# The relu sums of two batches on GpSimd instead of VectorE, in a fused attention and mixer kernel

## The chip, the cores and the metric

The kernel runs on one core of one Trainium2 chip. The metric is the device time of one execution in microseconds; the profile is of one execution.

## The reference

Attention with a window and a few global keys, then a mixer. q, k and v are 4 batches x 8 heads x 768 positions x 64 values in float32. What is computed, cut to its core:

```
scores = q @ k^T / sqrt(64) + bias(head, distance)   # kept: keys 0..7, and 0 <= row - key < 96
a      = softmax(scores);   x = (a @ v) with heads side by side   # 4 x 768 x 512
h      = x^T @ U @ V;       u = x + h^T                           # U 768x32, V 32x768
out    = u + relu(u @ w_ch1) @ w_ch2                              # 512 -> 2048 -> 512
```

## The kernel before

**Attention** goes by pairs of heads: 16 pairs, i = 4 b + pair. For a pair, `st_S` makes scores in PSUM (columns in three parts c = 0, 1, 2; VectorE adds the bias at L403), `st_E` the exponentials on ScalarE, `st_V(i, hi)` the product with the values. VectorE then scales that product into x_sb (L451) and GpSimd casts it to x16 in 16 bits (L452). `st_M1` multiplies x16 by U on TensorE (L461), `st_MT` turns the product (L478) and VectorE casts it (L479), `st_M3` multiplies by V (L515); VectorE adds that to x (L520), which is u, GpSimd casts it (L523), and a transposing DMA on the SP queue (`st_X`, L504) puts it into uT. GpSimd also casts each pair's v (`cast_v`, L142). VectorE copies a few columns into kA at L340.

**The mixer** goes by groups (b, g): three groups of 256 rows per batch. For batches 1 to 3 the second product is done with 7 products of quarters instead of 8. `mk_up` makes relu values: 8 units a group, each 8 matmuls (L629) and one relu on ScalarE into htr (L634). When half of a group's units are made, `queue_sums(k)` queues four sums of quarters of htr, 128x512 in 16 bits each, in the order s1, s2, s4, s3; s2 is made from s1, s4 from s2. k is 0 or 1, for the first and the second half. `mk_product` makes a product of 8 matmuls (L682) and adds it to x_sb (L687). The products come in the order x1, y1, x2, y2, x3, y3, x4; x2 uses s2, y2 s1, x3 s3, y3 s4, and the first four matmuls of a product use half 0 of a sum, the others half 1. Similar sums of quarters of w_ch2, named t1 to t4, are made once, early. Batch 0's mixer uses plain products (L664).

**The order** of all instructions on each engine is written out by hand. The main loop (from L800) goes over pairs, at a rate of one pair's attention for some nine units of the mixer; `fill(n)` issues n units (one `mk_up`, product or part of a plain product each). After each unit it raises `count` and takes one queued sum if that has become due (two, where more than four wait): a sum queued in a unit is due two units later. `need`, called by a product ahead of its matmuls, takes sums out of the queue until its own are issued. In the pair's step the fourth and fifth calls of `fill` stand behind `st_V(i - 1, 1)`, `cast_v(i)` and `st_S(i, 2)`, and ahead of `st_M1(i - 1)`. All engines work through their own instructions in that order.

Of the kernel before, what the change touches and what calls it, by code (L numbers as in the profile page):

```python
# [20 lines left out]
def kernel(  # L21
# [13 lines left out]
    nc = tc.nc  # L35
    B, H, S, D = q.shape
# [60 lines left out]
    def load_qk(i, behind=None):  # L97

        b, h0 = i // NP, 2 * (i % NP)
        got = []  # L100
        for src, nm in ((q, "qst"), (k, "kst")):
            st = stp.tile([P, 2, NSB, D], FP32, name=nm, tag=nm, bufs=2)
            if behind is not None:
                behind.memset(st[0:1, 0, 0, 0:1], 0.0)
            if i < NPE:
                nc.sync.dma_start(
                    st.rearrange("p h n d -> p h (n d)"),
                    src[b, h0:h0 + 2].rearrange("h (p n) d -> p h (n d)", n=NSB),
                )
            else:  # L110
                nc.sync.dma_start(
                    st.rearrange("p h n d -> p (h n) d"),
                    src[b, h0:h0 + 2].rearrange("h (n p) d -> p (h n) d", p=P),
                )
            got.append(st)
        staged[i] = got
# [10 lines left out]
    def cast_one(i, w, eng):  # L127
        st16 = stp.tile([P, NSB, 2, D], FP16, name=("q16", "k16")[w], tag=("q16", "k16")[w], bufs=2)
        eng.copy(st16.rearrange("p n h d -> p h n d"), staged[i][w])
        cast.setdefault(i, [None, None])[w] = st16  # L130

    def load_v(i):
        b, h0 = i // NP, 2 * (i % NP)
        st = stp.tile([P, 2 * NSB, D], FP32, name="vst", tag="vst", bufs=2)
        nc.sync.dma_start(
            st, v[b, h0:h0 + 2].rearrange("h (n p) d -> p (h n) d", p=P)
        )
        vsts[i] = st

    def cast_v(i):  # L140
        vt = vbuf[i % NVB]
        nc.gpsimd.tensor_copy(  # L142
            vt.rearrange("p n h d -> p h n d")[:, :, :, 0:D],
            vsts.pop(i).rearrange("p (h n) d -> p h n d", h=2),
        )
        vts[i] = vt
# [78 lines left out]
    def load_w1(c):  # L225
        js = slice(c * (DFF // 4), (c + 1) * (DFF // 4))
        nc.gpsimd.dma_start(w1_16[:, :, js], w1v[:, :, js])

    def load_w2(c):
        nc.gpsimd.dma_start(w2_16[:, 4 * c:4 * c + 4], w2v[:, 4 * c:4 * c + 4])  # L230
# [4 lines left out]
    def new_batch(b):  # L235
        xs[b] = xp.tile([P, NSB, DM], FP32, name="x_sb", tag="x_sb", bufs=3)
        tmps[b] = xp.tile([P, DM], FP16, name="tmp16", tag="tmp16", bufs=3)
        uTs[b] = xp.tile([P, NDC, S], FP16, name="uT", tag="uT")
# [60 lines left out]
    def st_A(i):  # L299
        vt = vts[i]  # L300
        vA = vap.tile([P, NSB - 1, 2, D + 1], FP16, name="vA", tag="vA")
        if i < NPE:
            nc.gpsimd.tensor_copy(vA, vt[:, 0:NSB - 1])
            vas[i] = vA
            return
        nc.sync.dma_start(vA[NG:P], vt[NG:P, 0:NSB - 1])
        nc.sync.dma_start(
            vA[0:NG].rearrange("p n h d -> p n (h d)"),
            vt[0:NG, 0:1].rearrange("p n h d -> p n (h d)").broadcast_to(
                (NG, NSB - 1, 2 * (D + 1))  # L310
            ),
        )
        vas[i] = vA
# [9 lines left out]
    def turn(i):  # L323
        stq, stk = cast.pop(i)
        qT = kp.tile([P, S], FP16, name="qT", tag="qT")
        kT = kp.tile([P, S], FP16, name="kT", tag="kT")
        nc.sync.dma_start_transpose(
            kT.rearrange("d (n p) -> d n p", n=NSB), stk.rearrange("p n h d -> p (n h d)")
        )
        nc.sync.dma_start_transpose(  # L330
            qT.rearrange("d (n p) -> d n p", n=NSB), stq.rearrange("p n h d -> p (n h d)")
        )
        qts[i] = qT
        kts[i] = kT
# [74 lines left out]
    def st_S(i, c):  # L409
        s_dve(i, scores(i, c, False))  # L410
# [138 lines left out]

    def queue_sum(name, part, out_, a, b_, op, wait=0):  # L550

        def go():
            nc.vector.tensor_tensor(out_, a, b_, op)  # L553
            have.add((name, part))
        (slow if name[0] == "t" else jobs).append((count[0] + wait, go))

# [29 lines left out]
    def queue_ff(b):  # L586
        for g in range(NFG):
            queue_group(b, g)
        if b == 0:
            for c in range(4):  # L590
                for made in first_ups:
                    ups_q.extend(made[2 * c:2 * c + 2])
# [118 lines left out]

    ahead, held, kept = [0], [True], deque()

    def fill(n):
        for _ in range(n):
            unit()
            count[0] += 1
            for _ in range(2 if len(jobs) > 4 else 1):
                for queue in (jobs, slow):
                    if queue and queue[0][0] < count[0]:  # L720
                        queue.popleft()[1]()
                        break

    def unit():
        down = downs_q and not held[0] and not any(place(w) <= place(downs_q[0][1]) for _, w in ups_q)
        room = ups_q and (not downs_q or place(ups_q[0][1]) - place(downs_q[0][1])
                          < (3 if held[0] else 2))
        if down and (ahead[0] > 0 or not room):
            ahead[0] = 0
            downs_q.popleft()[0]()  # L730
        elif room:
            ahead[0] = 1
            ups_q.popleft()[0]()
# [66 lines left out]
    for i in range(NP, NPAIR + 2):  # L800
        b, hp = divmod(i, NP)
        live = i < NPAIR
        units = iter(
            (0, 1, 1, 2, 1, 1, 1, 1, 1) if i == NP
            else (0, 1, 1, 1, 1, 1, 1, 1, 1) if i + 1 < NPE
            else (1, 1, 1, 2, 1, 1, 1, 1, 1)
        )
        held[0] = i < NP + 3
        if hp == 0 and live and b + 1 < B:
            new_batch(b + 1)  # L810
        if live and i > NP:
            st_S(i, 0)
        if NPE <= i + 1 < NPAIR:
            turn(i + 1)
        if i + 1 < NPAIR and i != NP + 2:
            load_v(i + 1)
        if i + 2 < NPE:
            load_qk(i + 2)
        fill(next(units))
        if NPE + 2 <= i + 2 < NPAIR:  # L820
            cast_one(i + 2, 1, nc.scalar)
        if NP < i <= NPAIR:
            st_V(i - 1, 0)
        if i == NP:
            load_w1(2)
        if i + 1 < NPE:
            st_T(i + 1)
        if i == NP:
            load_w1(3)
        fill(next(units))  # L830
        if live:
            st_S(i, 1)
        fill(next(units))
        if NP < i <= NPAIR:
            st_V(i - 1, 1)
        if live:
            cast_v(i)
            st_A(i)
        if NPE + 2 <= i + 2 < NPAIR:
            cast_one(i + 2, 0, nc.scalar)  # L840
        if NPE <= i + 3 < NPAIR and i != NP + 2:
            load_qk(i + 3)
        if i > NP + 1 and (i - 2) % NP == NP - 1:
            queue_ff((i - 2) // NP)
            ahead[0] = 1
        if i == NPAIR + 1:
            break
        fill(next(units))
        if live:
            st_S(i, 2)  # L850
        fill(next(units))
        if i > NP:
            st_M1(i - 1)
        else:
            for xo, o, rb in later:
                nc.vector.tensor_tensor(xo, o, rb, ALU.mult)
        if i == NP + 1:
            load_w2(0)
            load_w2(1)
        if i + 2 < NPE:  # L860
            cast_qk(i + 2, nc.gpsimd)
        if live:
            st_E(i, 0)
            if i < NPE:
                st_P(i)
        fill(next(units))
        if i >= NPE:
            for _ in range(min(2, len(kept))):
                kept.popleft()()
        if i > NP:  # L870
            st_MT(i - 1)
        if NPE <= i + 1 < NPAIR:
            st_K(i + 1)
        fill(next(units))
        if i > NP:
            st_M3(i - 1)
        if live:
            st_E(i, 1)
        fill(next(units))
        if i == NP + 1:  # L880
            load_v(i + 2)
            load_qk(i + 4)
        if i > NP:
            st_X(i - 1)
        if i == NP + 1:
            load_w2(2)
            load_w2(3)
        if NPE <= i + 2 < NPE + 2:
            cast_qk(i + 2, nc.gpsimd)
        fill(next(units))  # L890
# [38 lines left out]
```

## Time and profile before

| what | value |
| --- | --- |
| time, median of the runs (least, most) | 232.01 us (231.02, 558.6), 3 runs |
| profiled execution: time, span | 231.95 us, 230.2 us |
| TensorE busy | 220.5 us, 96% |
| VectorE busy | 159.8 us, 69% |
| ScalarE busy | 124.8 us, 54% |
| GpSimd busy | 73.9 us, 32% |
| mean granted TensorE clock | 1.00 |
| sums of relu values (L553, 72 on VectorE), the fastest | 0.41 us each |

The span runs from the first to the last instruction; the execution's own time lies 1.75 us above it. In the text PE is TensorE, PEld its loads of weights, DVE VectorE, ACT ScalarE, POOL GpSimd; L553 is line 553 of the kernel. A timeline row has its start in us from the span's start, its length in us, the engine, the line, the operation with output and inputs, and in brackets the idle time of that engine before it and what ended it. A group's row has the number of instructions, then busy us and mean ns, then the idle time before them. Idle time of an engine costs nothing in itself; time counts where TensorE waits.

### The profile page before, as it was taken

To read this page: it belongs to the slowest core of one execution; us is meant where nothing else is said; L and a number is where in the kernel's file an instruction comes from. 1 tells how busy PE (TensorE), PEld (TensorE's weight loads), DVE (VectorE), ACT (ScalarE), POOL (GpSimd) and SP (SyncE) were. 2 spreads that over 40 slices of the span, in tenths; PEclk is the share of its full clock that TensorE was granted. 3 is DMA by queue.
4 is the path that set the end of the run, shared out by engine and by line. 5 is a ranking of instruction groups with operands and counts; after the bars stand their busy time and mean duration, and the time that the engine had idled before them with its cause. 6 is when DMAs were issued, how large, how long until landed. Compare 5 with 4: busy or idle time off the path is not lost.

```text
span 230.2 us, 5875 instructions
## 1 busy us (share of the span) xinstructions
PE 220.5 (96%) x2418; PEld 171.1 (74%) x2420; DVE 159.8 (69%) x337; ACT 124.8 (54%) x193; POOL 73.9 (32%) x118
## 2 busy tenths in 40 slices
PE   7889999999999999999999999999999999999993
PEld 2445678788744445887888878888988888888882
DVE  3687866658577979597989897989764344444452
ACT  6676757776805253868485857292733434333320
POOL 6399928287553322123313131313111000000000
PEclk9999999999999999999999999999999999999999
DMA  6999999969998979897989993961221202010022
GB/s 188 288 290 245 260 278 188 313 135 163 195 194 181 207 174 251 192 245 175 257 221 196 245 202 99 119 184 28 86 71 36 94 0 94 0 65 28 9 85 93
DMA packets 86563, 36.68 MB, mean 159 GB/s; under 512 B 74152, under 2 KB 83592, under 8 KB 86536
## 3 DMA queue, kind: packets, MB, share of 16 engines
q1 hardware_dynamic: 81480, 32.01, 57.4%
q0 software_dynamic: 5056, 4.29, 12.7%
q8 instruction: 19, 0.31, 0.6%
q14 instruction: 8, 0.07, 0.1%
HBM read 27.46 MB, written 6.29 MB: 147 GB/s over the span
## 4 chain that ended last, share of the span: by engine, by line
PE 66%; DMA 11%; DVE 10%; POOL 4%; ACT 4%; issue 2%; SPq 1%; ACTq 0%; POOLq 0%
PE hps L629 25%; PE cx L682 13%; PE cy L682 10%; PE cps L664 8%; DMA w<-in_moe_w_ch_dram 6%; DMA vst<-in_v_dram 4%; DVE sp L403 3%; PE sc L365 3%; DMA qst<-in_q_dram 2%; ACT ep L415 2%; DVE x_sb L451 2%; PE ob L432 2%; PE sc L515 1%; DVE s L553 1%; PE ob L428 1%
## 5 line engine op out<-in xcount | busy, mean ns | idle before, releaser
L629 PE MATMUL hps<-uT,w 128*128 128x256 f16 x756 | 96.0, 273 | 0.0
L634 ACT ACTIVATE htr<-hps 128x512 f16<-128x512 f32 x96 | 56.4, 598 | 58.4 <-PE hps L629 58.1
L629 PEld LDWEIGHTS <-w 128*128 128x128 f16 x756 | 70.6, 98 | 9.9 <-issue 0.2
L403 DVE SCALAR_TENSOR_TENSOR sp<-sc,relcat 128x1024 f32<-128x1024 f32 (+1 forms) x36 | 40.7, 1131 | 9.1 <-ACT ep L415 4.8
L415 ACT ACTIVATE ep<-sp 128x1408 f16<-128x1408 f32 x24 | 33.1, 1380 | 0.7 <-DVE sp L403 0.6
L452 POOL CAST x<-x_sb 128x384 f16<-128x384 f32 x30 | 16.1, 538 | 48.5 <-DVE x_sb L451 44.3
L682 PEld LDWEIGHTS <-htr 128*128 128x128 f16 x288 | 27.6, 98 | 3.6
L687 DVE TENSOR_TENSOR x_sb<-cx,x_sb 128x256 f32<-128x256 f32 x36 | 15.2, 422 | 18.3 <-PE cx L682 17.7
L664 PE MATMUL cps<-w,htr 128*128 128x512 f16 x96 | 24.0, 379 | 0.4 <-DMA w<-in_moe_w_ch_dram 0.4
L523 POOL CAST x<-x_sb 128x768 f16<-128x768 f32 x12 | 11.0, 915 | 40.8 <-DVE x_sb L520 37.2
L682 PEld LDWEIGHTS <-s 128*128 128x128 f16 x216 | 20.2, 98 | 2.9 <-DVE s L553 0.6
L687 DVE TENSOR_TENSOR x_sb<-cy,x_sb 128x256 f32<-128x256 f32 x27 | 11.4, 422 | 12.5 <-PE cy L682 12.3
L365 PEld LDWEIGHTS <-kT 64*128 64x128 f16 x192 | 8.3, 93 | 13.7 <-issue 12.4
L451 DVE TENSOR_TENSOR x_sb<-ob,rcp 128x384 f32<-128x384 f32 x30 | 16.7, 557 | 1.0
L365 PE MATMUL sc<-qT,kT 64*128 64x128 f16 x192 | 16.8, 221 | 0.3 <-DVE x_sb L520 0.2
L432 PE MATMUL ob<-v,ep 128*128 128x65 f16 x192 | 16.5, 193 | 0.0
L432 PEld LDWEIGHTS <-ep 128*128 128x128 f16 x192 | 13.9, 98 | 2.3 <-issue 0.4
L142 POOL CAST v<-vst 128x768 f16<-128x768 f32 x16 | 14.0, 877 | 3.9 <-DMA vst<-in_v_dram 3.9
L428 PE MATMUL ob<-vA,ep 128*128 128x65 f16 x160 | 14.4, 194 | 0.4 <-DVE vA L316 0.2
L664 PEld LDWEIGHTS <-htr 128*128 128x128 f16 x96 | 8.4, 97 | 8.5 <-issue 0.5
L520 DVE TENSOR_TENSOR x_sb<-sc,x_sb 128x768 f32<-128x768 f32 x12 | 11.5, 955 | 4.6 <-PE sc L515 4.6
L372 PE MATMUL sc<-qT,kA 64*128 64x128 f16 x160 | 14.2, 217 | 0.3
(108 smaller groups left out, 311.1 us busy)
## 6 DMA issues: line engine op xcount, KB each, us to landing
qst<-in_q_dram SPq DMA_DIRECT2D x16, 384.0 KB, 4.6
kst<-in_k_dram SPq DMA_DIRECT2D x16, 384.0 KB, 6.3
vst<-in_v_dram SPq DMA_DIRECT2D x16, 384.0 KB, 4.5
out_dram<-x_sb SPq DMA_DIRECT2D x23, 256.0 KB, 3.1
w<-in_moe_w_ch_dram POOLq DMA_DIRECT2D x8, 512.0 KB, 9.0
vA<-v SPq DMA_DIRECT2D x8, 152.3 KB, 3.6
out_dram<-x_sb SPq DMA_DIRECT2D x2, 128.0 KB
uT<-x SPq DMA_TRANSPOSE x12, 3.1
```

Of the source, the lines that this page charges most:

```text
L365: nc.tensor.matmul(scs[hi][:, o:o + P], kT[r, kb * P:(kb + 1) * P], qT[r, kb * P:(kb + 1) * P], start=(o == 0 and not on_pe), stop=(o + P ...
L403: nc.vector.scalar_tensor_tensor(out=sps[i][:, :, c0:c0 + tot], in0=both[:, :, 0:tot], scalar=qk_scale / slope[2 * (i % NP)], in1=relfs[c0 ...
L415: nc.scalar.activation(eps[i][:, hi], sps[i][:, hi], AF.Exp, scale=slope[2 * (i % NP)])
L428: nc.tensor.matmul(ob[:, qi], ep[:, OF[qi - 1]:OF[qi - 1] + P], vA[:, qi - 1, hi], start=True, stop=False,)
L432: nc.tensor.matmul(ob[:, qi], ep[:, DG[qi]:DG[qi] + P], vt[:, qi, hi], start=(qi == 0), stop=True,)
L451: nc.vector.tensor_tensor(xo, ob[:, :, 0:D], rb, ALU.mult)
L452: nc.gpsimd.tensor_copy(x16, xo)
L629: nc.tensor.matmul(hps[:, k * FT:(k + 1) * FT], w1_16[:, dc, jt * P:(jt + 1) * P], uT[:, dc, ts], start=(dc == 0 and k == 0), stop=(dc == ...
L634: nc.scalar.activation(cell["htr"][:, 2 * jp:2 * jp + 2].rearrange("p j t -> p (j t)"), hps, AF.Relu)
L664: nc.tensor.matmul(cps, htr[:, jc, t * P:(t + 1) * P], w2_16[:, jc], start=(b > 0 and jc == 0), stop=(jc == NJC - 1),)
L682: nc.tensor.matmul(ps, cell[a][:, j], weight(w, j), start=(first and j == 0), stop=(done is not None and j == HJ - 1), skip_group_check=True,)
L687: nc.vector.tensor_tensor(x_sb[:, n, cs], ps, x_sb[:, n, cs], ALU.add)
```

## The change

The sums of relu values of batches 1 and 2 (`name[1] < B - 1`, B is 4) are issued on GpSimd; those of batch 3 and the sums of weights stay on VectorE. `fill` gets a second argument; two calls of the main loop pass False, and then no queued sum is taken after the unit.

```diff
     def queue_sum(name, part, out_, a, b_, op, wait=0):
 
+        eng = nc.gpsimd if name[0] != "t" and name[1] < B - 1 else nc.vector
+
         def go():
-            nc.vector.tensor_tensor(out_, a, b_, op)
+            eng.tensor_tensor(out_, a, b_, op)
             have.add((name, part))
...
-    def fill(n):
+    def fill(n, sums=True):
         for _ in range(n):
             unit()
             count[0] += 1
+            if not sums:
+                continue
             for _ in range(2 if len(jobs) > 4 else 1):
...
-        fill(next(units))
+        fill(next(units), False)
         if live:
             st_S(i, 2)
-        fill(next(units))
+        fill(next(units), False)
         if i > NP:
             st_M1(i - 1)
```

## The prediction

> **What bounds the kernel now.** I read the page first: busy times, then the groups by line, then the table of stretches, the waits from 88 us on, and the timeline around the sums.
>
> ```profile
> PE 220.5 (96%) x2418; PEld 171.1 (74%) x2420; DVE 159.8 (69%) x337; ACT 124.8 (54%) x193; POOL 73.9 (32%) x118
> ```
>
> TensorE is busy for 220.5 of 230.2 us. The sums that move exist from 96 us on, so what counts is how much TensorE waits there. The table of stretches has, after the stretch and its length, the busy time of PE, PEld, DVE, ACT and POOL:
>
> ```profile
> 111.00:122.00 11.00, 11.00 (x139) 9.26 (x135) 9.78 (x21) 8.03 (x12) 3.01 (x4) 1.00 0.95 230
> 122.00:133.00 11.00, 11.00 (x137) 9.33 (x137) 9.77 (x21) 7.54 (x11) 2.76 (x4) 1.00 1.07 223
> 133.00:145.00 12.00, 11.72 (x147) 9.55 (x145) 10.39 (x21) 7.54 (x11) 2.97 (x5) 1.00 0.68 141
> ```
>
> VectorE is busy for 9.8 of 11 us here and GpSimd for 3, which makes the move look cheap. But TensorE has no gap: from 89 to 220 us it idles 0.6 us in all. The waits (us in all, times, the longest) say which part of that VectorE's load causes:
>
> ```profile
> PEld L682 <- DVE s L553: 0.6, 1, 0.6
> PE cx L682 <- DVE s L553: 0.3, 1, 0.3
> PE sc L515 <- DVE tmp L479: 0.2, 1, 0.2
> ```
>
> One wait of TensorE for a sum (0.28 us; its weights came 0.56 us late) and one of 0.21 us for the cast at L479. Freeing VectorE can return about half a microsecond; any new wait of TensorE is paid in full.
>
> **What changes, part by part.**
>
> (1) 48 of the 72 sums (six groups of eight) move to GpSimd, those of batch 3 stay.
>
> ```profile
> L553 DVE TENSOR_TENSOR s<-htr 128x512 f16<-128x512 f16 x18 | 8.1, 453 | 3.3 <-ACT htr L634 3.3
> ...
> L294 POOL COPY kA<-kT 128x640 f16<-128x640 f16 x3 | 2.2, 722 | 5.0 <-DVE kT L277 5.0
> ...
> L195 POOL TENSOR_SCALAR rel<-relB 8x128 bf16<-8x128 f32 x1 | 0.5, 537 | 1.0 <-ACT rel L198 1.0
> ```
>
> VectorE sheds 48 x 0.46 = 22 us. No row has a two-operand operation on GpSimd, so its price **d** is bounded. Below: the undisturbed casts took 0.51 us for 384 elements and 0.83 us for 768, that is 0.19 us fixed and 0.83 ns an element (the copy of 640: 0.19 + 0.53 = 0.72, as measured). One operand of 512 would be 0.62 us. Above: the only arithmetic on GpSimd, L195, took 0.537 us for 128 elements; all of what exceeds 0.19 us taken per element (2.7 ns) gives 1.58 us. Between them, reading both operands one after the other at the copy's rate gives 0.19 + 2 x 0.43 = 1.04 us, and two whole passes 1.24 us. I take 1.15, between these two, since a sum is nearest to two copies. The Trainium skill (GPSIMD Engine Reference, Performance versus the Vector engine) speaks against the move: its two inputs share one read port, and 2048 elements take 4497 ns, so by an estimate from that 1.12 us here, which would lower the sum below by 0.4 us; no run so far shows it.
>
> (2) GpSimd works in order, and its casts stand in the same queue: two of 0.51 us a pair at L452 (their x16 feeds st_M1's U product), one of 0.84 at L142, one of 0.83 at L523. What counts is when the second operand half of product x2 is ready. Its eight matmuls use half 0 of s2, then half 1: the fifth starts 0.44 us after the first. Half 1 needs s1 and s2, one after the other: 2d.
>
> (3) The two fills that take no sums (between st_V hi = 1 and st_M1) shift the emission. I followed the counts: a unit raises `count`, a sum becomes due two units after its relu, one is taken a unit (two with over four waiting). In groups (1,0), (1,2) and (2,1) the s1 and s2 of half 1 fall due just in those two fills. They are skipped, and `need` then issues both directly ahead of x2. In GpSimd's queue they stand behind the second x16 cast and, in batch 1's two groups, behind cast_v. In (1,1) and (2,0) they come behind the L523 cast. Only (2,2), beside which no attention is left, has time: relu at 181.6, two sums to 183.9, x2's fifth matmul 184.8.
>
> ```profile
> 102.98 0.64 POOL L452 CAST x<-x_sb 128x384 f16<-128x384 f32 x1 [2.50 <-DVE x_sb L451]
> ...
> 103.86 1.03 PE L682 MATMUL cx<-t,s 128*128 128x256 f16 x8
> ...
> 118.85 0.95 POOL L523 CAST x<-x_sb 128x768 f16<-128x768 f32 x1 [3.59 <-DMA vA<-v]
> ...
> 120.95 1.03 PE L682 MATMUL cx<-t,s 128*128 128x256 f16 x8
> ...
> 135.87 0.51 POOL L452 CAST x<-x_sb 128x384 f16<-128x384 f32 x1 [1.93 <-DVE x_sb L451]
> 136.08 0.57 DVE L553 TENSOR_TENSOR s<-htr 128x512 f16<-128x512 f16 x1
> 136.32 1.03 POOL L142 CAST v<-vst 128x768 f16<-128x768 f32 x1
> ...
> 137.68 0.61 PE L682 MATMUL cx<-t,s 128*128 128x256 f16 x4 [0.28 <-DVE s L553]
> ```
>
> In the clock of before, with 2d = 2.30 and 0.04 us from an end to TensorE (s ended 137.63, the weights began 137.67):
>
> - (1,0): the x16 cast was ready 102.98 behind sums on VectorE; without them (1.0 us of them ahead of it) GpSimd is the limit: L523 to 96.92, s1 and s2 to 99.2, a cast from 99.6, s4 and s3 to 102.4. Cast to 102.9, cast_v to 103.75, sums to 106.05. x2's fifth matmul is due 104.30: **1.8 late**.
> - (1,1): L523 to 119.68, sums to 121.98, due 121.39: **0.6**.
> - (1,2): cast to 136.38, cast_v to 137.22, sums to 139.52, due 137.22: 2.3, less the 0.46 already lost there: **1.9**.
> - (2,0): L523 (start 152.90) to 153.73, sums to 156.03, due 155.44: **0.6**.
> - (2,1): cast (168.90) to 169.41, sums to 171.71, due 171.06: **0.7**.
>
> Each wait moves what follows by as much, so they add: 5.6, and 5 x 0.04 = 0.2, less the 0.21 us of L479's wait: **+5.6 us**. With d the sum moves as 12d - 8.2 from d = 0.95 up (two sums in four of the chains, four in that of (1,0)).
>
> (4) At no cost: s3 and s4 of half 1 run after x2's pair; x3 comes 3.5 us or more after x2, y3 5 us or more, against 2d = 2.3 for both and a cast. Of the casts ahead of M1, pair 9's starts when s3 ends at 102.4 and is done 0.8 us before M1 at 103.71; the other six meet no sum, since none is issued between them and M1 and the earlier ones are through. The casts of hi = 0 can be up to d late behind a sum, but M1 follows 3.6 us or more after their start. The transposes of st_X follow L523 on SP: pair 11's left SP 131.34 and group (2,0) first read uT at 135.54; s2 ahead of that cast ends before it is due, both move together, and the loads and stores behind it on SP move with TensorE. GpSimd issues no DMA after 54 us. t1 and t3 move by a unit or so on VectorE, long ahead of their use from 104 us on.
>
> The profiled execution took 231.95 us for a span of 230.2, and the median is 232.01. 232.0 + 5.6 = **237.6 us**. A measurement of this kernel can tell about 2%, 4.6 us, from no change; the sum is over that by 1.0 us.
>
> **The rivals.**
>
> (A) Not slower by 2%: GpSimd takes both operands at about the one-operand rate. It decides from d = 1.07 down (12 x 1.07 - 8.2 = 4.6). At d = 0.62 the waits of (1,1), (2,0), (2,1) are gone, (1,0) has 0.3 (the x16 cast is then bound by VectorE, 102.0) and (1,2) 0.8: +0.9, 232.9. For it: f16 and f32 copies cost the same per element, so bytes are not the limit. Against: L195 is dearer than a copy, and two operands are two reads.
>
> (B) GpSimd too slow for its queue: at d = 1.58 the x16 cast of pair 9 ends at 104.3, 0.6 late for M1 at 103.71, which takes its part of x2's wait; the formula gives 10.8, and further casts behind sums up to 1 us more: about 243. For it only L195, a shape on 8 partitions.
>
> (C) A new wait on VectorE: the kA copy at L340 (0.165 us, never beside a sum of GpSimd in this trace) is held by one. What shows such contention: sums of 0.41 us that overlapped a cast took 0.93 to 0.97, and casts went 0.51 to 0.64; L403 from PSUM beside a cast kept 1.23. L340 stands ahead of L520, which frees the sc bank for the next S; the bank is free 0.6 us early. One sum (at most 1.15, of which 0.8 is slack before M3 ends) costs nothing; two in a row cost 0.9 in five pairs: +4.5, 242. The Trainium skill (SBUF — State Buffer, Who interferes with whom) has such copies and GpSimd block each other for a whole instruction; the contended sums above agree with its case of two SBUF operands.
>
> (D) The relief of VectorE is all that shows: TensorE's waits of 0.46 and 0.21 go, 231.3. Against: the emission ahead of x2 is fixed by the counts.
>
> **From these the numbers.** The forecast 0.62 (d from 1.07 to 1.35: 236.6 to 240.0), A 0.19, B 0.10, C 0.07, D 0.02. Range: down into A to d = 0.9 (0.85 + 0.1 + 1.3 + 0.1 + 0.2 = +2.5), up to C's 242: 234.5 to 242. Slower by over 2%: forecast, B and C, 0.79; within 2%: A and most of D, 0.20; faster by over 2%: 0.01, as TensorE's waits from 96 us to the end hold too little for 4.6 us.
>
> **What would show it.** L553 on POOL with 48 instructions and a mean near 1.15 us; waits of PEld and PE at L682 (cx, weights t, operand s) for POOL s, five of them, two near 1.8 and three near 0.65 us; none at L461; DVE near 138 us; TensorE's busy time about the same in a longer span; from batch 3 on the same pace. I am wrong if L682's waits are absent or at other products, if a sum takes under 1 us, or if M1 (L461) or S (L365) waits.

## The result and the profile after

The changed kernel took 237.55 us (median of 4 runs, 236.87 to 238.82) against 232.6 (4 runs): a ratio of 1.0265, 95% interval 1.0222 to 1.0307. Every ratio here compares fast executions alone (the 558.6 us of before, 239.7 us of e5 and 238.11 us of e6 are not among them), so it is not the quotient of the two medians. The profiled execution took 238.82 us with a span of 237.0, 6.8 us over the span before. The lines below have numbers two higher from L553 on and four or more higher from L716 on; L682 is now L684, L687 L689.

Page, busy times, and groups of the sums on GpSimd and of the kA copy (the last row is the copy's group before the change):

```profile
PE 222.3 (94%) x2418; PEld 171.7 (72%) x2420; DVE 143.5 (61%) x289; ACT 124.9 (53%) x193; POOL 126.3 (53%) x166
...
L555 POOL TENSOR_TENSOR s<-htr 128x512 f16<-128x512 f16 x12 | 13.9, 1156 | 2.5 <-ACT htr L636 2.5
...
L340 DVE COPY kA<-kT 128x40 f16<-128x40 f16 x8 | 3.2, 400 | 0.0
```

```profile
L340 DVE COPY kA<-kT 128x40 f16<-128x40 f16 x8 | 1.3, 166 | 0.4 <-DMA kT<-k 0.4
```

The work has moved: GpSimd's busy time rises by 52 us, VectorE's falls by 16. A sum costs GpSimd 1.156 us, its four groups agree within 1 ns. The waits from 88 us on that TensorE and its weight loads have for GpSimd (there were none before):

```profile
PEld L684 <- POOL s L555: 6.6, 5, 2.4
...
PE cx L684 <- POOL s L555: 5.3, 5, 2.2
```

Five waits, all at cx with the operand s: x2. In three of the stretches TensorE idles 1.43, 0.53 and 2.16 us, where before it idled 0.21, 0 and 0.28 (the first row is the one of before that the prediction does not show):

```profile
100.00:111.00 11.00, 10.79 (x134) 8.88 (x132) 9.57 (x22) 7.21 (x11) 2.94 (x4) 1.00 0.87 199
```

```profile
100.00:111.00 11.00, 9.57 (x114) 7.94 (x112) 7.03 (x12) 7.79 (x12) 9.08 (x10) 1.00 0.97 232
...
122.00:133.00 11.00, 10.47 (x132) 8.61 (x129) 8.00 (x15) 7.30 (x11) 8.51 (x10) 1.00 0.91 197
133.00:145.00 12.00, 9.84 (x110) 7.51 (x104) 6.50 (x13) 5.33 (x9) 8.61 (x10) 0.87 0.77 164
```

The timeline around x2 of (1,0) and of (1,2), with the rows of GpSimd and of TensorE's product x2 alone:

```profile
102.44 0.50 POOL L452 CAST x<-x_sb 128x384 f16<-128x384 f32 x1
102.89 0.84 POOL L142 CAST v<-vst 128x768 f16<-128x768 f32 x1
103.68 1.15 POOL L555 TENSOR_TENSOR s<-htr 128x512 f16<-128x512 f16 x1
104.11 0.60 PE L684 MATMUL cx<-t,s 128*128 128x256 f16 x4
104.92 1.16 POOL L555 TENSOR_TENSOR s<-s,htr 128x512 f16<-128x512 f16 x1
106.13 0.61 PE L684 MATMUL cx<-t,s 128*128 128x256 f16 x4 [1.43 <-POOL s L555]
...
138.97 0.61 PE L684 MATMUL cx<-t,s 128*128 128x256 f16 x4
141.74 0.96 PE L684 MATMUL cx<-t,s 128*128 128x256 f16 x4 [2.16 <-POOL s L555]
```

The five pairs s1 and s2 stand in GpSimd's timeline where the prediction has them: behind the x16 cast and cast_v in (1,0) and (1,2), behind the cast of L523 in (1,1) and (2,0), behind the x16 cast in (2,1). Four matmuls of x2 run on half 0, the fifth stands until s2 of half 1 is made. What is lost is the time between the first and the fifth, less the 0.44 us of four matmuls: 106.13 - 104.11 - 0.44 = 1.58 us in (1,0), and by the same rows 0.69 in (1,1), 2.33 in (1,2), 0.70 in (2,0), 0.75 in (2,1); 6.05 in all. (The 5.3 us of the wait table leave out the end of the matmul ahead of it.)

The rest of the difference is the granted clock, which is 0.87 from 133 to 145 us. In smaller stretches of the same trace:

```profile
140.00:142.00 2.00, 0.26 (x2) 0.25 (x3) 0.03 (x1) 0.00 (x0) 1.84 (x3) 0.96 0.91 217
142.00:144.00 2.00, 2.00 (x17) 1.40 (x16) 0.42 (x1) 1.05 (x2) 2.00 (x2) 0.50 0.20 63
144.00:146.00 2.00, 2.00 (x17) 1.58 (x16) 0.44 (x3) 1.81 (x4) 0.03 (x1) 0.68 0.00 0
```

After the longest wait the clock is 0.50 and then 0.68: some 1.6 us lost (half of 2 us and a third of 2). What TensorE no longer loses to VectorE is 0.46 us at x2 of (1,2) and, at the two L515 whose operand L479 cast late, 0.37 and 0.29 us: before, L515 began 1.24 and 1.16 us after the start of the L629 unit ahead of it (106.03 - 104.79, 172.70 - 171.54), where it is 0.87 without a wait and in the trace after. Together: 6.05 of new waits, less 1.12, plus 1.6, and 0.25 from a later start of the whole stage (x2 of (1,0) begins at 104.11 instead of 103.86), 6.8 us, which is the difference of the spans.

Because the first 90 us vary from run to run, with the arrival of w_ch2 among other things (the wait for it is 0.4 us in the trace before, 1.4 after, 1.9 in e4), the profiles are compared below by their **stage**: from the start of the third product of (1,0) to the span's end. Before 230.2 - 103.86 = 126.3 us, after 237.0 - 104.11 = 132.9.

### The profile page after: what moved, and what is told of

Read it like the earlier page. It is cut to its first block, busy times and chain, and to the rows that moved or that the text cites. A ratio compares the mean times of both kernels' runs of the same rounds, so it can differ in the third digit from the quotient of the medians.

```text
span 237.0 us, 5884 instructions
## 1 busy us (share of the span) xinstructions
PE 222.3 (94%) x2418; PEld 171.7 (72%) x2420; DVE 143.5 (61%) x289; ACT 124.9 (53%) x193; POOL 126.3 (53%) x166
## 4 chain that ended last, share of the span: by engine, by line
PE 60%; POOL 16%; DMA 9%; DVE 7%; ACT 3%; issue 2%; SPq 1%; POOLq 0%; ACTq 0%
PE hps L631 23%; PE cx L684 12%; PE cy L684 8%; PE cps L666 8%; DMA w<-in_moe_w_ch_dram 6%; POOL s L555 5%; DMA vst<-in_v_dram 3%; DVE sp L403 2%; ACT ep L415 2%; PE sc L365 2%; POOL v L142 2%; POOL x L452 2%; DVE x_sb L451 1%; POOL q L123 1%; POOL vA L303 1%
## 5 line engine op out<-in xcount | busy, mean ns | idle before, releaser
L631 PE MATMUL hps<-uT,w 128*128 128x256 f16 x756 | 96.7, 274 | 0.0
L631 PEld LDWEIGHTS <-w 128*128 128x128 f16 x756 | 70.9, 98 | 10.0
L403 DVE SCALAR_TENSOR_TENSOR sp<-sc,relcat 128x1024 f32<-128x1024 f32 (+1 forms) x36 | 40.8, 1133 | 13.7 <-PE sc L365 5.3
L689 DVE TENSOR_TENSOR x_sb<-cx,x_sb 128x256 f32<-128x256 f32 x36 | 15.2, 424 | 29.7 <-PE cx L684 29.4
L684 PEld LDWEIGHTS <-htr 128*128 128x128 f16 x288 | 27.6, 98 | 3.6
L452 POOL CAST x<-x_sb 128x384 f16<-128x384 f32 x30 | 15.3, 511 | 25.8 <-DVE x_sb L451 20.5
L684 PEld LDWEIGHTS <-s 128*128 128x128 f16 x216 | 20.2, 99 | 9.2 <-POOL s L555 6.6
L523 POOL CAST x<-x_sb 128x768 f16<-128x768 f32 x12 | 10.4, 870 | 26.1 <-DVE x_sb L520 26.1
L689 DVE TENSOR_TENSOR x_sb<-cy,x_sb 128x256 f32<-128x256 f32 x27 | 11.4, 423 | 15.5 <-PE cy L684 15.0
L684 PE MATMUL cx<-t,s 128*128 128x256 f16 x72 | 10.6, 280 | 5.3 <-POOL s L555 5.3
L555 POOL TENSOR_TENSOR s<-htr 128x512 f16<-128x512 f16 x12 | 13.9, 1156 | 2.5 <-ACT htr L636 2.5
L142 POOL CAST v<-vst 128x768 f16<-128x768 f32 x16 | 13.4, 840 | 3.2 <-DMA vst<-in_v_dram 3.2
```

The source lines that it names most:

```text
L403: nc.vector.scalar_tensor_tensor(out=sps[i][:, :, c0:c0 + tot], in0=both[:, :, 0:tot], scalar=qk_scale / slope[2 * (i % NP)], in1=relfs[c0 ...
L452: nc.gpsimd.tensor_copy(x16, xo)
L555: eng.tensor_tensor(out_, a, b_, op)
L631: nc.tensor.matmul(hps[:, k * FT:(k + 1) * FT], w1_16[:, dc, jt * P:(jt + 1) * P], uT[:, dc, ts], start=(dc == 0 and k == 0), stop=(dc == ...
L684: nc.tensor.matmul(ps, cell[a][:, j], weight(w, j), start=(first and j == 0), stop=(done is not None and j == HJ - 1), skip_group_check=True,)
L689: nc.vector.tensor_tensor(x_sb[:, n, cs], ps, x_sb[:, n, cs], ALU.add)
```

## The experiments

The theory: five waits at x2, each for s1 and s2 of half 1, which run one after the other behind casts in GpSimd's queue. Rivals: the two fills that take no sums (1), and GpSimd's sums holding VectorE up, or GpSimd's load as such (2).

**e1: the move alone.**

```diff
-            if not sums:
-                continue
```

> The sums of batches 1 and 2 on GpSimd, but all calls of fill take sums, as before the change. My theory: the waits come from the order in GpSimd's own queue (s1 and s2 of half 1 behind the casts), and that order is the same with and without the two skipped fills, because nothing else is issued on GpSimd between the places. So the time is that of the changed kernel, 236.9 to 238, with five waits at x2. Rival 1, the skipped fills delay the sums: then the time falls back to 232 to 234. Rival 2, GpSimd's sums hold VectorE's instructions up (the kA copy took 1.14 us once): as my theory.

237.84 us (236.53 to 239.62), ratio 1.0256 (1.018 to 1.0332). The waits are the same five (PE 5.2 us), the stage 234.8 - 103.43 = 131.4. In the traces GpSimd's instructions stand in the same order as in the changed kernel. So for the moved sums the second half of the change does nothing: on GpSimd nothing else is issued between the skipped places and x2. Rival 1 falls.

**e2: the skipped fills alone, all sums on VectorE.**

```diff
-        eng = nc.gpsimd if name[0] != "t" and name[1] < B - 1 else nc.vector
+        eng = nc.vector
```

> All sums on VectorE, but the two fills take none. My theory: s1 and s2 of half 1 are issued straight ahead of x2 in groups (1,0), (1,2) and (2,1), behind the bias addition L403 of st_S, and cost VectorE 0.83 us there; TensorE waits up to 0.7 us at each: 232 to 234, at most 2 us over before. Rival 1 (the skipped fills are the cause): about 237. Rival 2 (the sums on GpSimd hold VectorE up): level with before, 231.5 to 232.5.

233.33 us (232.54 to 234.61), ratio 1.0068 (1.0039 to 1.0096). TensorE loses to VectorE's sums 0.75 us at x2 of (1,0) and 1.48 us at that of (1,2) (0.46 before); the profile's fifth matmuls start 1.19 and 1.92 us after the first. In (1,2):

```profile
137.16 0.61 PE L684 MATMUL cx<-t,s 128*128 128x256 f16 x4
...
137.27 0.96 DVE L403 SCALAR_TENSOR_TENSOR sp<-sc,relcat 128x768 f32<-128x768 f32 x1 [0.73 <-PE sc L365]
...
139.08 0.61 PE L684 MATMUL cx<-t,s 128*128 128x256 f16 x4 [1.31 <-DVE s L555]
```

Issuing the two sums late costs something where other work of the engine is issued in between, as st_S's addition (L403) is on VectorE; on GpSimd there is none. My range for the time held, and both rivals' did not; by place I was off, since (1,2) lost twice the 0.7 us that I allowed and (2,1) nothing.

**e3: cast_v and st_A one fill later, in all pairs.**

```diff
-        if live:
-            cast_v(i)
-            st_A(i)
...
         if live:
             st_E(i, 0)
-            if i < NPE:
-                st_P(i)
+        if live and i < NPE:
+            cast_v(i)
+            st_A(i)
+            st_P(i)
         fill(next(units))
+        if live and i >= NPE:
+            cast_v(i)
+            st_A(i)
```

> The changed kernel with cast_v and st_A issued one fill later, behind x2's sums instead of ahead of them. My theory: the waits of (1,0) and (1,2) shrink by the cast's 0.84 us each (1.58 to 0.75 and 2.33 to 1.5 us), those of (1,1), (2,0), (2,1) (0.7 each) stay: 1.7 us below the changed kernel, 235 to 236. Rival 1 (skipped fills): no difference. Rival 2 (VectorE held up): no difference, as GpSimd does the same work.

240.92 us (239.48 to 242.68), ratio 1.0387 (1.0314 to 1.046): missed. The waits did what was expected: (1,0) 108.78 - 107.73 - 0.44 = 0.61, (1,2) 1.55, and (1,1) none. But the stage began 3.6 us later than in the changed kernel, and a new wait took their place, for vA, which st_A's transfer brings:

```profile
51.51 0.28 DVE L316 COPY vA<-v 8x520 f16<-8x520 f16 x1 [3.98 <-POOL vA L303]
...
52.05 0.49 PE L515 MATMUL sc<-tmp,v16w 128*128 128x128 f16 x6 [2.58 <-DVE tmp L479]
...
127.91 0.23 PE L428 MATMUL ob<-vA,ep 128*128 128x65 f16 x1 [2.76 <-DMA vA<-v]
```

The later start comes mostly from a pair ahead of pair 8 (NPE is 8), where st_A is a copy on GpSimd (L303): it now stands behind the casts of q and k (L123) too, VectorE's L316 waits 3.98 us for it (0.97 in the changed kernel), and the cast of L479, behind L316 on VectorE, makes TensorE wait 2.58 us. The granted clock was 0.50 from 53 to 55 us, behind that wait, and again from 128 to 131 us, behind the other.

**e4: s1 and s2 of half 1 on VectorE, the other 36 sums on GpSimd.**

```diff
         eng = nc.gpsimd if name[0] != "t" and name[1] < B - 1 else nc.vector
+        if part == 1 and name[0] in ("s1", "s2"):
+            eng = nc.vector
...
-            if not sums:
-                continue
```

> As e1, but s1 and s2 of half 1 on VectorE: 36 of the 48 sums stay on GpSimd. My theory: x2's second half comes from VectorE after 0.83 us, as before the change, and all five waits for GpSimd go: 231 to 233, level with the kernel before, possibly 0.5 us under it since VectorE is less loaded. Rival 2 (GpSimd's sums hold VectorE up, or GpSimd's load as such): three quarters of the loss stays, 235.5 to 236.5.

231.4 us (10 runs, 230.43 to 232.75), ratio 0.9978 (0.995 to 1.0006): level with before. Three quarters of the sums stay on GpSimd (113 us busy) and TensorE no longer waits for it at x2; the one wait at x2 that remains is that of before, with the same length (this kernel's lines are two lower down again: L686 is L684 of the changed kernel, L557 its L555):

```profile
138.46 0.61 PE L686 MATMUL cx<-t,s 128*128 128x256 f16 x4 [0.28 <-DVE s L557]
```

The stage is 231.0 - 105.01 = 126.0, where before it was 126.3. The kA copies are still held for up to 0.94 us. So neither GpSimd's load nor its hold on VectorE makes the loss. The twelve sums that went back do, the first two of half 1 in six groups; those of (2,2) cost nothing in the changed kernel either.

**e5: y2 ahead of x2.**

```diff
-            for made in (x1, y1, x2, y2, x3, y3, x4):
+            for made in (x1, y1, y2, x2, x3, y3, x4):
```

> The changed kernel with the products in the order x1, y1, y2, x2, x3, y3, x4. My theory: what is late is the second of two sums in a row; y2 needs s1 alone, and x2 now comes two units (1.7 us and more) later. In (1,0) y2's fifth matmul waits 0.3 us for s1, in (1,2) 1.05 us, the others do not wait, x2 nowhere: 1.4 us of waits instead of 6.05, so 4.6 us under the changed kernel, 232 to 233.5. Rival (GpSimd's load or its hold on VectorE): no difference, since the same sums run there.

237.22 us (235.85 to 239.7), ratio 1.0238 (1.0189 to 1.0288): missed. The waits at y2 and x2 shrank as expected, but another came. (1,2), y2 and then x3:

```profile
137.40 0.61 PE L684 MATMUL cy<-t,s 128*128 128x256 f16 x4 [0.93 <-POOL s L555]
...
143.42 0.39 PE L684 MATMUL cx<-rel,htr 128*128 128x256 f16 x2 [1.81 <-POOL htr L555]
```

x3 uses s3, the last of the four, which stood behind the cast of L523 (141.43, waiting for M3) and ended at 143.36. Counting two sums was not enough: y2 in front put x3 directly behind x2, and then the third and fourth sum set the time. Stage 234.1 - 102.28 = 131.8, as in e1.

**e6: batch 2 alone on GpSimd.**

```diff
-        eng = nc.gpsimd if name[0] != "t" and name[1] < B - 1 else nc.vector
+        eng = nc.gpsimd if name[0] != "t" and name[1] == B - 2 else nc.vector
```

> Only batch 2's sums on GpSimd (24 instead of 48). My theory: the waits add by group, so (2,0) and (2,1) are left with 0.70 and 0.75 us, and (2,2) costs nothing. In batch 1 the sums are on VectorE with the two fills left out, which cost 1.6 us when all sums were there (233.3 against 231.7), mostly in (1,0) and (1,2). Sum: 231.7 + 1.4 + 1.0 to 1.6 = 234.1 to 234.7. Rival (GpSimd's load): half of the 5.7 us, 234.5 to 235; these two lie near each other, so the waits in the profile decide: two at x2 for GpSimd, 0.6 each.

234.31 us (233.66 to 238.11), ratio 1.0122 (1.0067 to 1.0177). The waits from 85 us on:

```profile
PEld L684 <- DVE s L555: 2.5, 2, 1.6
PE cx L684 <- DVE s L555: 1.9, 2, 1.3
PEld L684 <- POOL s L555: 1.7, 2, 0.9
PE cx L684 <- POOL s L555: 1.1, 2, 0.6
```

Two waits for GpSimd at (2,0) and (2,1), 0.70 and 0.76 us by the starts of the matmuls, as long as with 48 sums moved; (2,2) costs nothing. The other two are those of e2. The waits add by group.

**e7: cast_v and st_A at the head of the pair's step.**

```diff
+        if live:
+            cast_v(i)
+            st_A(i)
         if live and i > NP:
             st_S(i, 0)
...
-        if live:
-            cast_v(i)
-            st_A(i)
```

> The changed kernel with cast_v and st_A at the head of the pair's step, ahead of both x16 casts. My theory: as with the later cast_v, the waits of (1,0) and (1,2) shrink by 0.84 us (to 0.75 and 1.5), and now vA is not late, so no wait at L428 takes their place; waits below 1.6 us leave the clock at 1.00: 234.5 to 236. Rival: vA's two transfers or v's load are late in the new place and give it back, 237 or more.

237.22 us (236.47 to 238.52), ratio 1.0264 (1.022 to 1.0308): missed. (1,0) lost 1.17 us instead of 1.58, and (1,1) 1.24 instead of 0.69. From the L523 cast at 96.01 to the end of s2 at 105.33 GpSimd's timeline has no gap in this kernel, so a cast taken out of one place in that stretch and put into another moves the end by little: 9.32 us after the start of L523, against 106.08 - 96.34 = 9.74 in the changed kernel. And uT was late: TensorE waits for it 1.7 us in all at L631, in two places. At the second, its transpose left SP at 134.86, though its cast had ended at 133.06; in e1 it left as its cast ended (132.41 and 132.38). SP's transfers ahead of it, in another order here, held it; which of them is not shown. Where GpSimd's queue has a gap ahead of the casts, in (1,2), s2 ended at 140.71 and x2 no longer waited, but it began late itself. The rival's range held, though uT and not vA was late.

**e8: the longest wait filled.**

```diff
                 for j in range(HJ):
+                    if j == HJ // 2 and (b, g, a) == (1, 2, "s2"):
+                        busy = ps_ob()
+                        for _ in range(8):
+                            nc.tensor.matmul(busy, ident16, w1_16[:, 0, 0:512], start=True, stop=True)
```

> The changed kernel with 8 matmuls of 128x512 (0.22 us each, 1.74 us) that nothing uses, ahead of x2's fifth matmul in (1,2), where TensorE waits 2.3 us. Theory on the spread: the granted clock fell to 0.50 for about 3 us behind that wait in the profile of the changed kernel and not in that of e1, with the same wait; that costs 1.5 us when it happens. With the wait filled, TensorE idles 0.6 us there, the clock stays at 1.00, and all runs lie at 236 to 237.5, none at 238.5 and over. Rival (the clock falls by itself, whatever TensorE does): the same spread, 236.5 to 239.6.

236.72 us (6 runs, 235.94 to 237.11), ratio 1.0232 (1.0201 to 1.0264). Eight useless matmuls cost nothing: the wait ahead of the fifth matmul is 0.44 us instead of 2.16, and it starts 141.13 - 138.35 = 2.78 us after the first, as without them (2.77). No run reached 238.5. The stretch after the wait, here and in e1, where nothing was filled and the wait had the same 2.16 us:

```profile
142.00:144.00 2.00, 2.00 (x24) 1.83 (x23) 1.06 (x4) 2.00 (x4) 1.42 (x2) 1.00 0.00 0
```

```profile
142.00:144.00 2.00, 2.00 (x24) 1.84 (x22) 1.07 (x4) 2.00 (x4) 1.35 (x2) 1.00 0.00 0
```

Both have 1.00. So an idle of this length lowers the clock in some executions and not in others; the profiles of the changed kernel and of e10 show it, e1's does not. That filling the gap prevents it fits six runs of six within 1.2 us, against 3.1 us of spread in e1's four. The mean clock of each execution says the same: it is 0.993 in one of four of the changed kernel (238.82 us), two of four in e1 (239.62 and 238.88) and three of four in e10, and 0.999 or 1.00 in all six here. It is supported, not proved, all the more as one execution each of e5 (239.7) and e6 (238.11) has 0.993 too, though in the profiled executions of these two kernels no wait of TensorE is above 1.81 and 1.31 us; the two with the low clock were not profiled.

**e9: cast_v behind x2's sums in pairs 10 and 13 alone.**

```diff
-        if live:
+        if live and i not in (10, 13):
             cast_v(i)
             st_A(i)
...
         fill(next(units))
+        if i in (10, 13):
+            cast_v(i)
+            st_A(i)
```

> The changed kernel with cast_v and st_A issued behind x2's sums in pairs 10 and 13 alone, the two that stand ahead of (1,0) and (1,2). My theory: in e3 those two waits shrank as expected (1.58 to 0.61 and 2.33 to 1.55 us), and what made e3 slower was vA, late in other pairs (a wait of 2.76 us at L428 and time lost before 96 us). So here: (1,0) 0.6 to 0.75, (1,2) 1.5, no wait at L428, clock 1.00, 234.5 to 235.7, some 1.7 to 2.5 us under the changed kernel. Rival (the late cast costs vA its time in any pair): a wait at L428 of V(10) or V(13), 236.5 or more.

235.83 us (235.34 to 236.63), ratio 1.0193 (1.0153 to 1.0233): 0.1 us over my range, and under the rival's.

```profile
104.81 0.61 PE L684 MATMUL cx<-t,s 128*128 128x256 f16 x4 [0.63 <-POOL s L555]
...
139.88 0.61 PE L684 MATMUL cx<-t,s 128*128 128x256 f16 x4 [1.38 <-POOL s L555]
```

With the first matmuls at 103.59 and 137.89 that is 0.78 and 1.55 us: each 0.8 less, about the 0.84 us of one cast. The others stay (0.68, 0.69, 0.74), no matmul of V waits. The stage is 233.6 - 103.59 = 130.0, 1.4 under e1. That the order in GpSimd's queue is a cause is shown here: the casts and sums are the same, and in two pairs they change places.

**e10: the 128x40 copy on ScalarE.**

```diff
-        nc.vector.tensor_copy(
+        nc.scalar.copy(
             kA[:, :, 0:NG], kT[:, 0:NG].unsqueeze(1).broadcast_to((P, NSB - 1, NG))
         )
```

> The changed kernel with the 128x40 copy of L340 on ScalarE instead of VectorE. In the changed kernel it took up to 1.14 us beside GpSimd's sums, 0.17 before. My theory: nobody waits for VectorE there, so the five waits at x2 stay as they are and the time is that of the changed kernel, 236.5 to 238. Rival 2 (GpSimd's sums cost the time by holding VectorE up): 235 or less.

238.01 us (236.91 to 238.33), ratio 1.0267 (1.023 to 1.0303): no difference from the changed kernel, with the same five waits (PE 5.3 us). VectorE was held up (the copy's 0.17 us became as much as 1.14 in the changed kernel) and nobody paid for it.

**e11: e4 with half 1's sums due at once.**

```diff
-                queue_sum((name, b, g), k, ..., op, wait=0 if last else 2)
+                queue_sum((name, b, g), k, ..., op, wait=0 if last or (k and b < B - 1) else 2)
```

> e4 (s1 and s2 of half 1 on VectorE, 36 sums on GpSimd, level with before at 231.4), with half 1's sums due at once instead of two units later. My theory: e4's last wait for a sum, 0.28 us of TensorE and 0.46 in all at (1,2)'s x2, goes as well, and the rest stays as in e4: 0.3 to 0.6 us under the kernel before, a ratio of 0.997 to 0.999. It can't be much more, since TensorE has no other gap from 96 us to the end of the products. Rival: s1 ahead of st_V's scaling delays x16, and M1 (L461) waits: 232 or more.

233.73 us (6 runs, 233.12 to 233.98), ratio 1.0088 (1.0062 to 1.0115): missed, by a rival near the one named. x2 waits nowhere, but the early s1 of half 1 waits on VectorE for its relu, and the cast of L479 stands behind it:

```profile
117.31 0.42 DVE L557 TENSOR_TENSOR s<-htr 128x512 f16<-128x512 f16 x1 [2.43 <-ACT htr L638]
...
117.65 0.28 DVE L479 CAST tmp<-ob 128x128 f16<-128x128 f32 x1
...
117.99 0.49 PE L515 MATMUL sc<-tmp,v16w 128*128 128x128 f16 x6 [1.23 <-DVE tmp L479]
```

That happens twice, 2.5 us in all. The two units of delay in `queue_sum` are there for the relu. No version tried beats the kernel before by more than its runs can tell.

## Why the prediction was right

**The bound.** That VectorE's load had little to give back: shown by e4, where VectorE is relieved by 11 us, TensorE waits for GpSimd at no x2, and the time is level.

**The price of a sum.** Forecast 1.15, measured 1.156. The casts' rate gave 1.04 and 1.24 for two readings of the operation; that 1.15 between them was right to 1% is partly luck, and no run shows why the operation takes what it takes. The bound from L195 (1.58) was far off; the estimate of 1.12 from the figure of the Trainium skill (GPSIMD Engine Reference, Performance versus the Vector engine) was 3% low. Two in a row take 2.40 us (103.68 to 106.08), 0.1 us over the forecast's 2d of 2.30, since s2 starts 1.24 us after s1 there.

**The five places.** All five waits are where the emission was followed to, at half 1 of s2, and (2,2) has none. By place, forecast (from its times, with 0.04 for the hand-over) and measured: (1,0) 1.79 and 1.58; (1,1) 0.63 and 0.69; (1,2) 2.34 and 2.33; (2,0) 0.63 and 0.70; (2,1) 0.69 and 0.75. Their sum is 6.08 against 6.05. From batch 3 on the pace is that of before: from x2 of (2,2) to the end 45.8 us in both traces.

**What was wrong in it.** Part (3) has the skipped fills as the reason that s1 and s2 are issued straight ahead of x2. That is how they are issued, but e1 shows that it does not matter on GpSimd: the queue's order is the same without them. The step should have compared the order in that engine's queue, not the place of the call.

**What was missed.** VectorE's busy time, forecast near 138 us, is 143.5: the sums' groups fell by 23.1 us and the kA copy's rose by 1.9, but the spans of neighbouring instructions overlap, and the page counts the overlap once. The relief of VectorE returned 1.12 us to TensorE, and the sum had 0.67: the wait table shows 0.21 us for L479, and the second place, 0.29, not at all. The clock: the profiled execution (238.82 us, mean clock 0.993) lost 1.6 us to it, which the sum did not have, and TensorE's busy time grew by 1.8 us with it. The median does not hold this loss, since the other three executions have a mean clock of 1.00 and took 236.87 to 237.69. Without it the waits and the relief make 6.05 - 1.12 = +4.9 us, and e1's profiled execution, at a clock of 1.00, has a stage 5.0 us longer than before.

That the median met the forecast to 0.05 us is luck. The five terms add to +5.4 as they stand; rounding each to a tenth made +5.6. The relief was larger than the sum had it, executions of the changed kernel at a clock of 1.00 differ by 0.8 us, and the base of 232.01 us comes from three runs, where 41 later runs of that kernel have medians of 231.18 to 231.74 us in three series. From 232.01 the median rose by 5.5 us; of that 0.6 us is not accounted for by the waits and the relief. The places of the waits, their causes and their sum were right.

**The rivals.** (A) and (B) fall with the price. (C) happened in its first part only: the copies were held, up to 1.14 us, and at no cost, as the text had for a hold of one sum (e10). (D) falls with the result: the relief is there, 1.12 us, under 6.05 us of new waits.

## What to carry to other kernels

An engine that is busy for 3 of 11 us can still be the wrong place for work that another engine waits for: what counts is what stands ahead of it in that engine's queue, and how long the chain is that the consumer needs (here two sums in a row, 2.4 us on GpSimd, and 0.86 on VectorE in e2). Before moving work, list for each consumer what its operand's queue holds ahead of it, and move only the parts whose consumer comes late enough; e4 kept 36 of 48 sums on GpSimd at no cost, and with no gain that its runs can tell. A cure that swaps two items in a queue has to be followed one consumer further: e3, e5 and e11 each removed the wait that they aimed at and paid at the next one.

## What the runs showed of the hardware

A sum of 128x512 f16 with two operands on GpSimd takes 1.156 us, 2.8 times the 0.416 to 0.424 us of VectorE's in the same trace. From start to start it is 1.11 us when the next instruction does not use the result (142.87 after 141.76) and 1.23 when it does (140.53 after 139.30).

TensorE's granted clock fell to 0.50 behind one idle of 2.16 us at x2 of (1,2) in the profiles of the changed kernel and of e10, and behind those of 2.58 and 2.76 us in e3, and came back to 1.00 within some 4 us; behind the same 2.16 us in e1 it stayed at 1.00, as it did in the profiles behind every loss of 1.6 us and less at x2. The Trainium skill (TensorE: Matmul & The Clock Gate, Part 1: The HAM clock gate) has the clock halve after an idle window of about 3.4 us; here about two thirds of that was enough in some executions, and the measurement decides.

Beside GpSimd's two-operand sums, VectorE's small copy from SBUF to SBUF was held for up to 1.14 us, while the bias addition with one operand in PSUM kept its time (L403: 1131 ns before, 1133 after).
